# Gated linear attention feeding a two-layer feed-forward block: five hidden tiles in another form, a small copy on another engine, and a new first part of a written order

## The chip, the cores and the metric

One core of a Trainium2 chip runs the whole program. The metric is device time in microseconds (us), the median of several executions. The engines are named as in the profile: PE (TensorE, matmuls), PEld (its weight loads), DVE (VectorE), ACT (ScalarE), POOL (GpSimd), SP (SyncE, which issues nearly all transfers here).

## The reference, cut to what matters

```python
batch, n_heads, seq, head_dim = (4, 8, 768, 48)      # tokens: 3072, d_model 384, d_ff 2048
f = 1.0 / (1.0 + np.exp(-f_logit))
for t in range(S):
    state = f[:, :, t, :, None] * state + np.einsum('bhd,bhe->bhde', k[:, :, t], v[:, :, t])
    y[:, :, t] = np.einsum('bhd,bhde->bhe', q[:, :, t], state)
x = np.ascontiguousarray(attn_out.transpose(0, 2, 1, 3)).reshape(B * S, H * D)
h = x @ w_in
relu6 = np.clip(h + 3.0, 0.0, 6.0)
g = h * relu6 / 6.0
return (g @ w_out).astype(np.float32)
```

## The kernel before, in words

**Attention** is done in 24 units: a unit is 128 tokens of one batch entry, unit i belongs to token block i // 4. Each unit has a chain of small steps, named by a token `step.i`: `gate` (ACT, sigmoid), `back` (DVE, a scan that gives the product of the gates from each position to the end of the chunk), `kmul`, `rend` (DVE, the inverse of the whole chunk's product), `fwd` (DVE, a scan the other way that overwrites the first one's tile), `qmul`, then on PE `tk`, `att`, `kv`, `qs`, `av` with `ktok`, `mask`, `carry0`, `carry1`, `decay` between them, and `xh`, `xs`, `xl`, which leave the result as two float16 parts. `rend` first writes the chunk's product into the tile `ends`, clipped from below (L444, `tensor_scalar_max`), then its inverse (L445). `ends` is read later by `decay` and at the end of the program.

**Feed-forward.** The 2048 hidden values are 16 tiles of 128. A token block has 512 tokens, and one token `op.n` is tile n mod 16 of block n // 16. Float32 numbers are carried as a float16 high and low part. The first product `mm1` is 9 matmuls in float16 (three split products, three parts of the inner size). `relu` (ACT) and `g` (DVE) make the hidden value in float32, `gh` (ACT, L683) its high part, `gl` (DVE or POOL, L693) its low part, and `mm2` (L709) adds 9 float16 matmuls into three PSUM tiles `o`. In the first block, while attention still fills the machine, some tiles take another form:

- tiles 0 to 4: the 512 tokens in two halves, `mm1a` and `mm1b` (L828), `relua`/`relub`, `ga`/`gb`, and as second product `mm2a`/`mm2b` (L846), three matmuls each in float32 on the unsplit hidden value and the unsplit weights;
- tiles 5 to 7: whole tiles, with a float32 second product `mm2x` (L720), three matmuls; these need no `gh` and no `gl`;
- tiles 8 to 15 and later blocks: the split form above.

The weights are loaded by `ld` (SP) and turned into the two parts by `z`, `cy`, `high` (ACT) and `mid`, `dif`, `top`, `low` or `lowi`/`lowo` (DVE or POOL). From token block 2 on the first product is done in another way (L772, L801, L806); the change leaves it alone.

**Order.** A written list, `ORDER`, of some 1,560 tokens fixes the order on every engine and on the SP queue: each engine does its instructions in that order, and waits where an input isn't there. `ON_POOL` lists the tokens whose elementwise work goes to POOL rather than DVE. A token `warm.n` is n idle matmuls of 128 columns on PE (L1071). `outv.1` is the first token from which on the list is the same before and after, but for the inserted `ends` tokens. In the trace of before it begins at 121.18 us on DVE, and PE's next piece there, `mm1.23`, at 120.41 us.

Of the kernel before, what the change touches and what calls it, by code (L numbers as in the profile page):

```python
# [58 lines left out]
z.0 mid.0 loadq.2 gate.3 back.3 ld.1 carry0.1 warm.1 qs.1.0 dif.0 kmul.2 top.0 fwd.2 xl.0 carry1.1 loadq.3 av.1 hole.0
tk.2.4 rend.3 xh.1 xs.1 xl.1 z.1 qmul.2 warm.5 att.2.2 kmul.3 cy.1 mid.1 fwd.3 ktok.2 loadv.2 high.0 warm.4 kv.2.1  # L60
carry0.2 tk.3.4 ktok.3 mask.2 load.4 gate.4 qs.2.0 hole.1 av.2 xh.2 carry1.2 lowi.0 mm1a.0.4 relua.0 dif.1 qmul.3
top.1 high.1 ga.0 loadv.3 xs.2 att.3.2 mask.3 kv.3.1 ld.2 carry0.3 carry1.3 lowi.1 xl.2 loadq.4 warm.1 qs.3.2 av.3
xh.3 mm1a.1.4 cy.2 xs.3 xl.3 relua.1 z.2 back.4 kmul.4 rend.4 fwd.4 ga.1 decay.4 mm2a.0 qmul.4 load.5 gate.5 tk.4.1
mm2a.1 ktok.4 loadv.4 ld.3 cy.3 z.3 hole.2 mid.2 dif.2 top.2 att.4.2 kv.4.3 hole.3 mm1b.0.0 high.2 back.5 mid.3
relub.0 loadq.5 mm1b.1.1 relub.1 lowi.2 gb.0 dif.3 kmul.5 rend.5 gb.1 mm1a.2.4 mm1b.2.0 top.3 mm2b.0 mm2b.1 fwd.5
tk.5.1 relua.2 relub.2 gb.2 qmul.5 ld.4 z.4 cy.4 mid.4 mm2b.2 high.3 ktok.5 lowi.3 ga.2 mm1b.3.0 load.6 gate.6 loadq.6
dif.4 back.6 top.4 load.7 mm1a.3.4 ld.5 relub.3 mm2a.2 relua.3 ga.3 high.4 gb.3 cy.5 z.5 mask.4 mm2a.3 lowi.4 mm1a.4.1
relua.4 rend.6 ld.6 mm1b.4.4 relub.4 loadv.6 gate.7 loadq.7 mm2b.3 carry0.4 kmul.6 fwd.6 mid.5 ga.4 dif.5 z.6 qmul.6
top.5 cy.6 tk.6.1 ktok.6 mm2a.4 back.7 ld.7 decay.5 high.5 qs.4.2 decay.6 att.5.0 gb.4 av.4 kv.6.1 carry1.4 lowi.5
mm1.5.4 mask.5 mm2b.4 carry0.6 xh.4 z.7 xl.4 mid.6 dif.6 kmul.7 carry1.6 loadv.5 kv.5.3 ld.8 relu.5 g.5 mm2x.5 cy.7  # L70
top.6 high.6 cy.8 rend.7 tk.7.0 mid.7 dif.7 load.8 lowi.6 carry0.5 top.7 mm1.6.4 ktok.7 qs.5.2 fwd.7 qmul.7 high.7
loadv.7 relu.6 g.6 z.8 decay.7 att.6.0 ld.9 lowi.7 gate.8 av.5 cy.9 z.9 mask.6 mm1.7.4 relu.7 mid.8 dif.8 top.8 mid.9
carry1.5 dif.9 high.8 low.8 mm2x.6 mm1.8.0 g.7 loadq.8 ld.10 top.9 xh.5 cy.10 relu.8 high.9 back.8 rend.8 mm2x.7 ld.11
xl.5 g.8 att.7.2 z.10 cy.11 qs.6.0 kv.7.3 mid.10 load.10 loadv.8 av.6 dif.10 low.9 top.10 z.11 mid.11 gh.8 mm1.9.4
ld.12 ld.14 xh.6 xl.6 gl.8 mm2.8 dif.11 high.10 low.10 relu.9 g.9 cy.12 mm1.10.1 top.11 mask.7 kmul.8 carry0.7 gh.9
gl.9 hole.4 relu.10 high.11 mm2.9 carry1.7 g.10 low.11 z.12 mid.12 ld.13 dif.12 top.12 cy.13 gh.10 gl.10 tk.8.1 ktok.8
mm1.11.0 z.13 high.12 qs.7.2 mm2.10 av.7 loadq.9 ld.15 kv.8.3 decay.8 relu.11 mid.13 dif.13 low.12 loadv.9 mm1.12.1
g.11 gh.11 xh.7 top.13 carry0.8 high.13 xl.7 hole.7 gl.11 relu.12 z.14 z.15 low.13 fwd.8 qmul.8 mm2.11 g.12 gh.12
mm1.13.4 relu.13 g.13 cy.14 gh.13 gl.13 gl.12 mm2.12 cy.15 qs.8.2 mid.14 dif.14 att.8.0 mask.8 lowo.0 top.14 high.14
hole.6 hole.5 mm1.16.4 load.9 mid.15 mm1.17.1 relu.16 carry1.8 relu.17 dif.15 ws1.0 g.16 mm1.20.0 g.17 loadq.11 low.14  # L80
gate.10 xtop.0 gate.9 mm1.18.1 load.11 top.15 relu.18 loadq.10 back.9 high.15 gh.16 av.8 back.10 mm1.14.4 g.18 mm2.13
lowo.4 gh.17 relu.14 low.15 g.14 gh.14 mm1.15.1 mm1.19.4 lowo.6 gh.18 kmul.9 gl.18 rend.9 relu.15 g.15 lowo.3 gh.15
gl.14 gl.15 tk.9.1 lowo.5 lowo.1 mm2.14 fwd.9 mm2.15 gl.16 ktok.9 gl.17 outs.2 loadv.11 lowo.7 outv.1 outs.0 mm1.23.1
mm2.16 gate.11 lowo.2 ws2.0 relu.19 od.0 ws3.0 mm2.17 rend.10 xh.8 g.19 back.11 od.2 kmul.10 relu.20 decay.9 relu.23
kmul.11 hole.8 fwd.10 rend.11 od.1 load.13 qmul.10 xsum.0.2 g.20 g.23 mm1.21.4 relu.21 load.12 xleast.0 tk.10.3 ws4.0
qmul.9 decay.10 ktok.10 mm2.18 gh.19 g.21 mm1.25.3 gh.20 mm1.24.2 gh.21 loadv.10 gate.12 wtop.4 gl.19 relu.24 att.9.1
relu.25 kv.9.0 gl.20 fwd.11 g.25 carry0.9 loadv.12 g.24 wsh.0 load.14 qmul.11 mm1.22.4 gate.13 relu.22 back.12 gh.24
mm2.19 tk.11.3 gl.21 ws1.1 mask.9 gh.23 carry1.9 ktok.11 mm2.20 g.22 qs.9.0 att.11.3 gate.14 loadq.12 gh.25 gl.25 av.9
att.10.2 mm2.21 back.13 gh.22 xh.9 gl.23 kv.11.0 rend.12 kv.10.1 gl.22 mask.10 loadq.13 decay.11 mm1.26.4 ws2.1
mask.11 carry0.10 qs.10.3 ws3.1 carry0.11 carry1.10 kmul.12 kmul.13 fwd.12 qs.11.1 av.10 av.11 relu.26 mm2.22 ws4.1  # L90
xh.10 xh.11 decay.12 rend.13 mm1.27.3 gl.24 carry1.11 relu.27 loadq.14 decay.13 fwd.13 tk.12.2 mm1.28.1 relu.28 hole.9
ktok.12 wsl.0 ws1.2 g.27 tk.13.0 mm2.23 qmul.12 qmul.13 wsh.1 hole.10 att.13.3 ws2.2 g.26 ktok.13 g.28 xtop.1 att.12.1
t0.4 loadv.13 kv.12.2 kv.13.0 back.14 carry0.13 load.15 hole.11 load.16 xsum.1.4 carry0.12 gh.26 mm2.24 gh.27 mm2.25
t0.5 mask.13 carry1.12 t1.4 t1.5 seed.0.2 kmul.14 mm1.30.3 gh.28 t2.4 ws3.2 xleast.1 carry1.13 t2.5 th.4 ws4.2 gate.15
mask.12 gl.26 gl.27 wsl.1 th.5 ws1.3 mm2.26 tl.4 mm1.29.1 tk.14.2 relu.30 mm1.31.0 tl.5 relu.29 rend.14 g.30 p1.8.4
loadv.14 ktok.14 ws2.3 relu.31 p7.8.2 g.29 wsh.2 cs.8 ca.8.2 loadv.17 mm2.27 g.31 p6.8 gh.29 gate.16 fwd.14 qs.13.0
xtop.2 cx.8.3 qs.12.1 p2.8 wsl.2 ws3.3 ra.8 back.15 gl.28 p5.8 av.13 av.12 mm2.28 gh.31 gaw.8 loadq.15 loadq.17 gh.30
ws4.3 rend.15 load.17 ce.8 wsh.3 p4.8 qmul.14 gl.30 gl.29 xh.13 xh.12 p3.8 p8.8 rb.8 rx.8 p7.9.1 decay.14 wsl.3 mm2.29
# [1140 lines left out]
```

## Time and profile before

| | |
|---|---|
| median of 3 runs | 459.32 us (459.2 to 459.85) |
| the profiled execution's own time | 459.1 us |
| its span, first to last instruction | 457.4 us |
| outside the span | 1.7 us |
| granted TensorE clock | 1.00 of 2.4 GHz |

The profiled execution lies 0.2 us under the median. A busy PE at a granted clock of 1.00 is not yet a PE without gaps; the durations of its pieces have to be read as well.

### The profile page before, as it was taken

How to read it: one execution, taken by the hardware profiler on the slowest of the kernel's cores; microseconds unless marked ns; L12 is line 12 of the kernel's file. 1: busy time of each engine (PE TensorE's matmuls, PEld its weight loads, DVE VectorE, ACT ScalarE, POOL GpSimd, SP SyncE). 2: the span in 40 equal slices, each digit the busy share in tenths (PEclk: the TensorE clock that was granted, in tenths of full speed). 3: DMA queues.
4: the chain of work that ended last, by engine and by line, in shares of the span. 5: the costliest groups of instructions: out<-in, count | busy, mean ns of one | idle time of the engine just before them, and what ended most of it. 6: DMA issues, size and time to landing. Idle time of an engine off the chain costs nothing.

```text
span 457.4 us, 12555 instructions
## 1 busy us (share of the span) xinstructions
PE 449.4 (98%) x5445; PEld 292.8 (64%) x5449; DVE 359.3 (79%) x643; ACT 231.2 (51%) x389; POOL 19.0 (4%) x31
## 2 busy tenths in 40 slices
...
GB/s 283 223 251 385 225 189 251 203 155 16 52 125 99 158 52 59 108 3 120 89 1 85 78 142 18 21 143 2 1 10 1 5 29 2 1 115 2 1 0 73
DMA packets 25531, 43.18 MB, mean 94 GB/s; under 512 B 2560, under 2 KB 17408, under 8 KB 25472
## 3 DMA queue, kind: packets, MB, share of 16 engines
...
q14 instruction: 16, 0.13, 0.1%
...
## 4 chain that ended last, share of the span: by engine, by line
PE 94%; DVE 2%; DMA 1%; ACT 1%; issue 0%; SPq 0%; ACTq 0%
PE o L709 35%; PE pair L772 16%; PE single L772 9%; PE pair L664 7%; PE single L664 5%; PE o L846 3%; PE pair L497 3%; PE pair L587 3%; PE pair L571 3%; PE pair L537 2%; PE o L720 2%; PE pair L516 2%; PE o_half L862 1%; PE pair L862 1%; PE single L828 1%; PE pair L828 1%
## 5 line engine op out<-in xcount | busy, mean ns | idle before, releaser
L709 PE MATMUL o<-gg,weight 128*128 128x512 f16 x744 | 173.5, 379 | 0.1
L709 PEld LDWEIGHTS <-weight 128*128 128x128 f16 x744 | 71.7, 98 | 73.8
L772 PEld LDWEIGHTS <-weight 128*128 128x128 f16 x672 | 65.1, 98 | 13.3 <-issue 0.2
L772 PE MATMUL pair<-xmem,wide 128*128 128x256 f16 x384 | 51.2, 273 | 0.1
L683 ACT ACTIVATE gg<-raws 128x512 f16<-128x512 f32 x64 | 38.4, 624 | 23.9 <-DVE raws L806 8.1
L772 PE MATMUL single<-xmem,weight 128*128 128x256 f16 x384 | 49.8, 273 | 0.2 <-DVE raws L806 0.2
L801 ACT ACTIVATE raws<-pair,half 128x512 f32<-128x512 f32 x32 | 21.5, 684 | 42.7 <-PE pair L772 33.7
L772 PEld LDWEIGHTS <-wide 128*128 128x128 f16 x384 | 36.9, 98 | 8.7 <-DVE single L787 0.6
L801 ACT ACTIVATE raws<-single,half 128x512 f32<-128x512 f32 x32 | 22.0, 687 | 40.0 <-PE single L772 32.4
L664 PEld LDWEIGHTS <-weight 128*128 128x128 f16 x243 | 23.1, 98 | 26.8 <-issue 0.3
L772 PE MATMUL pair<-xmem,weight 128*128 128x256 f16 x288 | 36.5, 273 | 0.0
L806 DVE SCALAR_TENSOR_TENSOR raws<-raws,single 128x512 f32<-128x512 f32 x32 | 21.8, 682 | 18.4 <-ACT raws L801 18.4
L693 DVE TENSOR_TENSOR gg<-raws,gg 128x512 f16<-128x512 f32 x48 | 31.9, 682 | 5.0 <-ACT gg L683 5.0
L664 PE MATMUL pair<-xmem,weight 128*128 128x512 f16 x144 | 33.2, 379 | 0.0
L787 DVE TENSOR_TENSOR pair<-pair,raws 128x512 f32<-128x512 f32 x16 | 11.2, 697 | 25.5 <-PE pair L772 17.2
L806 DVE SCALAR_TENSOR_TENSOR raws<-raws,pair 128x512 f32<-128x512 f32 x32 | 21.5, 681 | 12.3 <-ACT raws L801 12.1
L448 DVE TENSOR_TENSOR_SCAN suffix<-gates,rend 112x516 f32<-112x516 f32 x24 | 29.7, 1236 | 0.1
L428 DVE TENSOR_TENSOR_SCAN suffix<-gates,unit 112x516 f32<-112x516 f32 x23 | 28.1, 1224 | 0.5 <-ACT gates L422 0.5
L664 PE MATMUL single<-xmem,weight 128*128 128x512 f16 x99 | 23.2, 380 | 0.1
L674 ACT ACTIVATE tg<-pair,half 128x512 f32<-128x512 f32 x16 | 10.9, 687 | 19.5 <-PE pair L664 16.3
L683 ACT ACTIVATE gg<-tg 128x512 f16<-128x512 f32 x24 | 14.4, 626 | 9.1 <-DVE tg L678 5.2
L504 DVE TENSOR_TENSOR a<-pair,causal 128x512 f32<-128x512 f32 x24 | 16.3, 682 | 1.2 <-PE pair L537 1.2
...
## 6 DMA issues: line engine op xcount, KB each, us to landing
...
```

The source lines that it names most:

```text
L428: nc.vector.tensor_tensor_scan(flat(sf)[:, ::-1], gt[:, 1:][:, ::-1], flat(unit)[:, ::-1], 0.0, op0=ALU.mult, op1=ALU.add,)
L448: nc.vector.tensor_tensor_scan(flat(sf), gt[:, :NP * (C + 1)], flat(rend), 0.0, op0=ALU.mult, op1=ALU.add,)
L497: nc.tensor.matmul(d["at"][HC * odd:HC * (odd + 1), e, 2 * n + c], t[rs, 1, n, c, odd], t[rs, 0, n, c, odd], start=not growing[at], stop=T ...
L504: nc.vector.tensor_tensor(d["a"].rearrange("r p e t -> r e p t"), d["at"], causal.unsqueeze(1).unsqueeze(1).broadcast_to([128, 2, NP, HC]) ...
L571: nc.tensor.matmul(d["y"][to:to + 64, odd, n, cs], before[rs, p], t[rs, 0, n, c, odd], start=alone and (odd, e) not in seen, stop=False, s ...
L664: nc.tensor.matmul(h, win[:, f, a, k * 128:(k + 1) * 128], g["xt"][:, k, :g["n"] // C, b], start=i == 0, stop=i == 3 * KT - 1,)
L683: nc.scalar.activation(d["gg"][:, 0], d["t"], AF.Copy)
L693: engine("gl", int(g["name"]) * NF + f).tensor_tensor(d["gg"][:, 1], d["t"], d["gg"][:, 0], op=ALU.subtract)
L709: nc.tensor.matmul(g["o"][m], wout[:, f, a, m * 128:(m + 1) * 128], g[f]["gg"][:, b], start=f == 0 and i == 0, stop=f == NF - 1 and i == 2 ...
L772: nc.tensor.matmul(to[:, n * 256:(n + 1) * 256], weights(q, n, a), g["wide"][:, :, block - 3, b], start=fresh and count == 1, stop=count = ...
L801: nc.scalar.activation(to, src, AF.Relu, bias=half, scale=RISE)
L806: nc.vector.scalar_tensor_tensor(to, to, TOP, src, op0=ALU.min, op1=ALU.mult)
```

## The change

Tiles 3 to 7 of the first block take the split form (`mm1`, `relu`, `g`, `gh`, `gl`, `mm2`) in place of the halves (3 and 4) or the float32 second product (5 to 7). The copy of the chunk's product into `ends` goes to ACT as a step of its own, without the clip; DVE's inverse reads the scan's result directly. The list before `outv.1` is another one; `ON_POOL` has 5 tokens in place of 15. Lines from 445 on move by 2 to 4.

```diff
 ON_POOL = """
-kmul.1 decay.4 kmul.6 lowi.5 kmul.7 decay.7 lowi.7 kmul.8 gl.9 decay.8 gl.11 qmul.8 gl.12 lowo.0 low.14
+lowi.2 gl.3 lowo.5 qmul.6 low.9
 """.split()
 ORDER = """
...
+mm1.6.4 ktok.7 qs.5.2 fwd.7 qmul.7 high.7
...
+        def close():
+            nc.scalar.activation(ends[:, i], sf[:, :, 0], AF.Copy)
+
         def turn():
-            nc.vector.tensor_scalar_max(ends[:, i], sf[:, :, 0], END_LIMIT)
-            nc.vector.reciprocal(rend[:, :, 0], ends[:, i])
+            nc.vector.reciprocal(rend[:, :, 0], sf[:, :, 0])
...
-            "kmul": kmul, "rend": turn, "fwd": forward,
+            "kmul": kmul, "ends": close, "rend": turn, "fwd": forward,
```

On PE, at the second product of tile 5 (`tg_5` is its float32 hidden value, `gg_5` its two float16 parts, `o` the three output tiles, `wide` the unsplit and `weight` the split weights), before:

```order
L537 MATMUL pair_71<-v_912,ktok_714 48x48
L720 MATMUL o_0_572<-tg_5_931,wide 128x512
L720 MATMUL o_1_573<-tg_5_931,wide 128x512
L720 MATMUL o_2_574<-tg_5_931,wide 128x512
L516 MATMUL pair_70<-ident,qkf_792 128x112 x4
```

and now the first six of eighteen rows, three rounds of them in all:

```order
L713 LDWEIGHTS weight
L713 MATMUL o_0_622<-gg_5_924,weight 128x512
L713 LDWEIGHTS weight
L713 MATMUL o_1_623<-gg_5_924,weight 128x512
L713 LDWEIGHTS weight
L713 MATMUL o_2_624<-gg_5_924,weight 128x512
```

Three float32 matmuls have become nine float16 ones, which also wait for `gg`.

On DVE, the rows up to the second `ga` (the 37th to 48th row of its program in both), that is the end of the start-up (L428 is `back`, L448 `fwd`, L841 `ga`, L301, L308 and L312 `mid`, `dif`, `top` of a weight tile, L441 `kmul`, L504 `mask`, L320 a low part), before:

```order
L308 TENSOR_TENSOR top_377<-top_377,raws 128x768
L454 TENSOR_TENSOR qkf_325<-qkf_325,suffix_77 112x512
L312 SCALAR_TENSOR_TENSOR wide<-top_377,wide 128x2x384
L841 SCALAR_TENSOR_TENSOR th_0_461<-th_0_461,single 128x256
L504 TENSOR_TENSOR a_488<-pair_71,causal 128x2x4x64
L320 TENSOR_TENSOR weight<-wide,weight 128x384
L428 SCALAR_TENSOR_TENSOR suffix_79<-gates_78,unit 112x516
L441 TENSOR_TENSOR qkf_519<-qkf_519,suffix_79 112x512
L444 TENSOR_SCALAR ends<-suffix_79 112x4
L445 RECIPROCAL rend<-ends 112x4
L448 SCALAR_TENSOR_TENSOR suffix_79<-gates_78,rend 112x516
L841 SCALAR_TENSOR_TENSOR th_1_562<-th_1_562,single 128x256
```

and now (line numbers 2 to 4 higher):

```order
L310 TENSOR_TENSOR top_408<-top_408,raws 128x768
L443 TENSOR_TENSOR qkf_373<-qkf_373,suffix_79 112x512
L314 SCALAR_TENSOR_TENSOR wide<-top_408,wide 128x2x384
L449 RECIPROCAL rend<-suffix_79 112x4
L303 TENSOR_SCALAR raws<-top_542 128x768
L452 SCALAR_TENSOR_TENSOR suffix_79<-gates_78,rend 112x516
L310 TENSOR_TENSOR top_542<-top_542,raws 128x768
L322 TENSOR_TENSOR weight<-wide,weight 128x384
L314 SCALAR_TENSOR_TENSOR wide<-top_542,wide 128x2x384
L845 SCALAR_TENSOR_TENSOR th_0_589<-th_0_589,pair_70 128x256
L458 TENSOR_TENSOR qkf_373<-qkf_373,suffix_79 112x512
L845 SCALAR_TENSOR_TENSOR th_1_616<-th_1_616,pair_70 128x256
```

The steps of a third weight tile (`top_542`) and the `qmul` of unit 4 have come ahead of the second `ga`, and the first `ga`, which was the fourth of these rows, is now the tenth.

On ACT, the start of its program after the first two sigmoids, before:

```order
L422 ACTIVATE gates_78<-gates_78 112x4x128
L523 ACTIVATE ktok_156<-pair_71 128x448
L550 ACTIVATE middle_102<-pair_70 112x2x2x48
L422 ACTIVATE gates_80<-gates_80 112x4x128
L608 ACTIVATE xmem<-pair_71 112x4x128
L523 ACTIVATE ktok_243<-single 128x448
```

and now:

```order
L446 ACTIVATE ends<-suffix_77 112x4
L424 ACTIVATE gates_78<-gates_78 112x4x128
L527 ACTIVATE ktok_162<-single 128x448
L446 ACTIVATE ends<-suffix_79 112x4
L424 ACTIVATE gates_80<-gates_80 112x4x128
L424 ACTIVATE gates_76<-gates_76 112x4x128
L554 ACTIVATE middle_102<-pair_71 112x2x2x48
```

The copies (L446) stand between the sigmoids, and the sigmoid of the fourth unit (the second `gates_76`) has moved ahead of the first `carry0` (`middle_102`).

## Rows read from the trace of the kernel before

**Rows 1.** Page, part 1: engine, busy us (share of the span), instructions.

```profile
PE 449.4 (98%) x5445; PEld 292.8 (64%) x5449; DVE 359.3 (79%) x643; ACT 231.2 (51%) x389; POOL 19.0 (4%) x31
```

**Rows 2.** Windows: length, busy (instructions) of PE, PEld, DVE, ACT, POOL, clock, DMA.

```profile
3.50:31.30 27.80, 25.09 (x581) 16.94 (x580) 25.56 (x42) 16.37 (x32) 2.05 (x3) 1.00 0.80 296
31.30:121.20 89.90, 89.90 (x1034) 54.36 (x1033) 81.95 (x142) 61.73 (x95) 14.41 (x14) 1.00 0.50 182
121.20:250.00 128.80, 128.64 (x1812) 81.40 (x1812) 118.45 (x213) 64.49 (x112) 0.00 (x0) 1.00 0.27 84
```

**Rows 3.** Chain that ended last, 30 to 82 us: start, us, what.

```profile
32.95 1.48 PE o L846 x6
...
35.06 0.44 PE pair L537 x26
...
37.57 0.98 PE single L828 x9
...
39.53 2.59 PE o L846 x12
...
67.98 2.58 PE o L720 x6
70.55 1.94 PE pair L664 x9
...
79.10 1.94 PE o L709 x9
```

**Rows 4.** Lines by form, DVE, 31.3 to 121.2 us: count, busy us, mean ns, idle before.

```profile
L312 DVE SCALAR_TENSOR_TENSOR wide<-top,wide 128x768 int16<-128x768 int16 x14 | 14.3, 1024 | 0.1
L308 DVE TENSOR_TENSOR top<-top,raws 128x768 int16<-128x768 int16 x14 | 7.8, 555 | 0.3
...
L320 DVE TENSOR_TENSOR weight<-wide,weight 128x384 f16<-128x384 f32 x10 | 5.4, 553 | 0.2 <-ACT weight L317 0.2
L693 DVE TENSOR_TENSOR gg<-tg,gg 128x512 f16<-128x512 f32 x8 | 5.3, 683 | 0.8 <-ACT gg L683 0.7
L301 DVE TENSOR_SCALAR raws<-top 128x768 int16<-128x768 int16 x14 | 4.9, 350 | 0.1
L678 DVE SCALAR_TENSOR_TENSOR tg<-tg,single 128x512 f32<-128x512 f32 x7 | 4.8, 685 | 3.4 <-ACT tg L674 3.4
...
L841 DVE SCALAR_TENSOR_TENSOR th<-th,single 128x256 f32<-128x256 f32 x4 | 1.6, 410 | 0.3 <-ACT th L837 0.3
L441 DVE TENSOR_TENSOR qkf<-qkf,suffix 112x512 f32<-112x512 f32 x2 | 1.4, 684 | 0.0
...
L444 DVE TENSOR_SCALAR ends<-suffix 112x4 f32<-112x4 f32 x5 | 0.8, 162 | 0.0
L457 DVE TENSOR_TENSOR decayed<-state,ends 112x192 f32<-112x192 f32 x2 | 0.7, 350 | 0.0
```

**Rows 5.** Timeline of DVE, 112 to 123 us: start, us, what.

```profile
116.24 1.29 DVE L693 TENSOR_TENSOR gg<-tg,gg 128x512 f16<-128x512 f32 x2
```

**Rows 6.** Timeline of all engines, 0 to 36 us.

```profile
2.98 0.20 ACT L253 ACTIVATE table<-half 128x1 f32<-128x1 f32 x1 [0.89 <-POOL half L251]
...
8.05 1.23 DVE L428 TENSOR_TENSOR_SCAN suffix<-gates,unit 112x516 f32<-112x516 f32 x1 [0.51 <-ACT gates L422]
...
9.50 1.42 POOL L441 TENSOR_TENSOR qkf<-qkf,suffix 112x512 f32<-112x512 f32 x1 [5.76 <-DMA qkf<-qk]
...
9.79 1.16 DVE L444 TENSOR_SCALAR ends<-suffix 112x4 f32<-112x4 f32 x1
...
27.24 0.42 DVE L841 SCALAR_TENSOR_TENSOR th<-th,single 128x256 f32<-128x256 f32 x1 [0.97 <-ACT th L837]
```

**Rows 7.** Waits of DVE, 31.3 to 121.2 us: waited for, us in total, times, longest.

```profile
DVE tg L678 <- ACT tg L674: 4.5, 6, 2.4
```

**Rows 8.** Timeline of PE, 118 to 124 us.

```profile
120.41 2.11 PE L664 MATMUL pair<-xmem,weight 128*128 128x512 f16 x9
```

More of the change, by code (lines that the diff above doesn't have):

```diff
@@ L59 @@
[L59 to L98, printed above, removed]
@@ new lines @@
+top.2 ga.0 loadq.6 gate.5 qmul.4 warm.1 relua.1 ga.1 cy.3 z.3 mm2a.0 back.5 decay.4 mid.3 cy.4 mm2a.1 gate.6 carry0.4
+z.4 dif.3 carry1.4 mm1b.0.0 top.3 carry1.3 ends.5 back.6 high.3 lowi.3 mid.4 mm1b.1.1 ld.5 att.4.2 relub.0 gb.0 load.7
+dif.4 mm1.3.4 ends.6 high.2 ld.6 kmul.5 relub.1 mask.4 lowi.2 relu.3 gb.1 mm2b.0 loadv.5 rend.5 mm1a.2.0 top.4 fwd.5
+z.5 cy.5 high.4 mid.5 mm1b.2.2 qmul.5 lowi.4 ld.7 tk.5.3 mm1.4.1 g.3 lowo.3 relua.2 dif.5 relub.2 mm2b.1 gate.7
+loadq.7 gh.3 relu.4 ld.8 cy.6 gb.2 ga.2 mm2b.2 g.4 loadv.6 top.5 z.6 ktok.5 mid.6 qs.4.0 gl.3 kmul.6 high.5 dif.6 gh.4
@@ new lines @@
+decay.5 top.6 back.7 att.5.3 lowi.5 cy.7 ld.9 high.6 kv.5.1 av.4 z.7 carry0.5 mask.5 tk.6.4 cy.8 mm2a.2 mm2.3 lowo.6
+mid.7 mm1.5.2 kmul.7 z.8 dif.7 lowo.5 lowo.4 lowi.6 mid.8 top.7 ktok.6 relu.5 high.7 mm1.6.3 g.5 gh.5 gl.4 lowi.7
+mm2.4 rend.6 cy.9 loadv.8 z.9 carry1.5 gl.5 dif.8 relu.6 decay.6 loadq.8 top.8 fwd.6 tk.7.2 mid.9 ld.10 xh.4 mm1.7.4
+ktok.7 relu.7 g.6 high.8 z.10 gh.6 qmul.6 loadv.7 g.7 dif.9 low.8 mm2.5 gl.6 cy.10 rend.7 ends.7 top.9 high.9 fwd.7
+qs.5.1 att.6.3 kv.6.2 carry0.6 mask.6 ld.11 av.5 ld.12 carry1.6 low.9 xl.4 load.9 mm1.8.4 mid.10 cy.11 loadq.9 xh.5
```

130 lines of the change are left out of this document (81 added, 49 removed).

## The prediction

> **What bounds the kernel now.** I read the page's busy times first: PE is busy 98% of the span, DVE 79% [rows 1]. A mean over the span hides the stages, so next the windows [rows 2]. From 31.3 to 121.2 us, the stretch in which the new list takes effect after the start-up, PE is busy 89.90 of 89.90 us: there is no gap in it to win, only work to take out. DVE, second, is busy 81.95 us of it, so it has 7.95 us to spare. Behind 121.2 us PE is again full (128.64 of 128.80) and DVE at 118.45. Before 31.3 us things are different: PE works 25.09 of 27.80 us, part of it idle matmuls, and DVE 25.56; there the chain of the first attention units sets the pace, and DVE is its busiest engine. The chain that ended last [rows 3] runs from 31 us on through one matmul group after another. So the reader should look for three things: how much PE work goes, what the start-up gives, and whether DVE, which takes over work, can follow.
>
> **PE work that goes.** A float32 second product takes 2.58 us whole and 2.59 us in two halves; the split one takes 1.94 us [rows 3]. The two half-size first products take 0.98 us each, the whole one 1.94: no difference. Three tiles give 3 x 0.64 us and two give 2 x 0.65 us: **3.2 us** less on PE, which has nothing to hide it under in this stretch. The rows are of the same shapes, so I give this term no range.
>
> **The start-up.** Its end is the second `ga` on DVE, which frees PE's second `mm2a` (at 32.95 us, [rows 3]). Pieces on DVE that follow each other overlap a little: two low parts of 0.683 us take 1.29 us together [rows 4, 5], so each further one costs its mean less 0.08 us. Ahead of that `ga` there come in, by [rows 4]: `kmul.1` from POOL 0.60, `mid` 0.27, `dif` 0.47, `top` 0.94 of the third weight tile, and `qmul.4`, of the shape of `kmul`, 0.60: 2.9 us. Out go five `ends` pieces, four of 0.16 us and one that took 1.16 us: 1.8 us. Two waits also end: 0.51 us of the second unit's scan, since `qmul.0` now stands ahead of it, and 0.97 us of the first `ga`, which now comes six pieces later [rows 6]. Net the second `ga` comes 2.9 - 1.8 - 1.5 = -0.4 us, so 0.4 us earlier. PE has by then also done `kv.4` (0.44 us, [rows 3]), which stood behind it. I take **0.8 us**. Lower bound -0.7: both waits come back elsewhere. On the SP queue, one v load of 128 x 400 floats has moved ahead of the second unit's q and k; at 296 GB/s [rows 2] it delays them by 0.7 us, from the 9.50 us at which POOL got them [rows 6] to 10.2 us. DVE comes to `kmul.1` at about 10 us by the sum of the pieces before it, so this costs at most some 0.3 us, inside the bound. The later loads move to earlier places among pieces that wait for them less than in the list of before; I cost them at nothing, under the cover of DVE's own queue.
>
> PE alone would thus come to `mm1.23` at 120.41 [rows 8] - 3.2 - 0.8 = 116.4 us: a limit of 4.0 us.
>
> **What DVE takes on.** Up to `outv.1` it does 7 more `gl` (five tiles more, two fewer on POOL: 15 for 8) at 0.60 us, 4 more `kmul` at 0.60, 3 more `decay` at 0.27, one more `lowi` at 0.47; four half-size `ga`/`gb` of 0.33 become two whole `g` of 0.60 (-0.1); ten `ends` go, nine at 0.16 and one at 1.16 us (-2.6) [rows 4, 6]. That is 4.2 + 2.4 + 0.8 + 0.5 - 0.1 - 2.6 = **+5.2 us**. From 3.5 to 121.2 us DVE was busy 25.56 + 81.95 = 107.5 of 117.7 us and idle 10.2 us. To arrive 4.0 us earlier it must do 112.7 us of work in 113.7 us: 1.0 us of idle time is left. The start-up keeps some 0.75 us (2.24 less the 1.5 above), so 0.25 us remains for a stretch that had 7.95.
>
> That price is between two ends. If DVE never waits longer than that, the gain is 4.0 us. If it waits there as long as before, and PE waits for every bit, the gain is 4.0 - 7.7 = -3.7 us. The largest part of those waits, 4.5 us in six pieces, is DVE at `g` waiting for ACT's `relu` of a matmul group just done [rows 7]: the wait of an engine that is ahead of PE. With 98% of its time full DVE is mostly behind, and such waits shrink. So I take the value near the first end: 1.7 us of idle time, which costs **1.5 us**.
>
> **What is cheap.** The copy into `ends` has no row on ACT. The nearest are ACT's 128 x 1 piece at 0.20 us [rows 6] and DVE's 112 x 192 `decay` at 0.35 us [rows 4]; I take 0.2, it is that small. Ten copies and five `gh` (no longer than `gl`, 0.68 us) are 5.4 to 7 us more on an ACT that idles 28 of 89.9 us [rows 2]. The cover is this idle time; if it were gone, each copy would delay the `relu` or sigmoid behind it by 0.2 us. The Trainium skill speaks against this part: in "ScalarE: Activation LUTs", "Rules for kernel authors", it gives relu, max, min, add and mul to VectorE and budgets about 0.3 us for every activation. By that an estimate for 24 copies is 7.2 us, by the row 4.8 us, and either fits in ACT's idle time.
>
> The `ends` piece of 1.16 us began while POOL's `kmul.1` ran, and ended with it, at 10.95 and 10.92 us [rows 6]; the same piece alone takes 0.16. I count this 1.0 us as gone, since that POOL piece is. If it were chance, and came back on another piece, the sum would be 1.0 us worse. By the Trainium skill ("SBUF — State Buffer", "Who interferes with whom") it isn't chance: VectorE and GpSimd share a port pair, and the second to come is blocked until the first has finished; the trace agrees at this place.
>
> Behind `outv.1` PE's work is the same and full, DVE loses fourteen `ends` (2.2 us) and has 10.35 us to spare up to 250 us [rows 2], in which it can work off a lag. I take nothing there, bounds -0.4 and +0.4 us.
>
> **Sum.** 3.2 + 0.8 - 1.5 = 2.5 us off the profiled execution's 459.1 us: 456.6. The median of before lies 0.2 us higher, so for a median I say **456.8 us**.
>
> **Rivals.**
> - *DVE eats the gain.* At about 4.2 us of idle time on DVE between 31 and 117 us, half of what was there, nothing is left: 459.3. For it: work and time on PE and DVE now match to 1 us. Against: the waits seen are those of an engine ahead.
> - *DVE becomes the bound and the kernel is slower.* DVE is in order; each time it comes to `g` before ACT's `relu` is there, everything behind it, now also `gl`, `kmul` and `decay`, is late, and with them the low parts that the last third of each `mm1` and `mm2` reads. It decides from 4.2 us up; with the whole 7.95 us it gives 459.3 + 3.7 = 463.0. POOL, which took some of this load, is used for 5 pieces instead of 15.
> - *The scan waits for the copy.* `fwd` overwrites the tile that ACT's copy reads, so it must wait for ACT's queue up to the copy; behind `fwd` DVE's whole queue stands. If each of ten early copies sat behind one piece of 0.7 us, DVE would lose 7 us, near the rival before: some 461 to 462. Against: in the list other DVE pieces (`kmul`, `qmul`, `mid`) stand between `rend` and `fwd` in nearly every unit, and ACT is the less busy engine.
> - *No waits at all*: 455.3.
>
> **How the numbers follow.** I give the forecast (a gain of 1 to 3.9 us: 455.4 to 458.3) 0.65, the eaten gain 0.18, DVE as the bound 0.10, the scan behind the copy 0.04, no waits 0.03. The range 455.0 to 460.2 leaves out the two slower cases' far ends and little else, under 2 in 10; the forecast's own is 455.4 to 458.3. A difference of 0.2%, 0.9 us, is about the least that this measurement can tell. Faster than that: the forecast and no waits, 0.68. Within: 0.18. Slower: 0.14.
>
> **What would show it.** Right: tiles 3 to 7 with nine matmuls of 1.94 us in all, no float32 group after tile 2; PE at `mm1.23` between 116.5 and 119 us and full from 32 us on but for 1 to 2 us; DVE over 97% busy in that stretch, with `g` waiting for ACT under 2.5 us; the second `mm2a` before 32.95 us; from `outv.1` to the end the same 336.2 us within 0.5. Wrong: idle time on PE between 32 and 117 us of over 3 us released by DVE's low parts, `kmul` or `qmul`; `fwd` waiting for ACT; a start-up whose second `mm2a` comes after 33.5 us; a granted clock under 1.00 anywhere.

## The result

The changed kernel is 0.8% slower: 462.88 us (461.56 to 463.0, 4 runs) against 459.26 us (4 runs), a ratio of 1.0077 with a 95% interval of 1.0065 to 1.0090. The forecast was 456.8 us, faster. The profiled execution took 461.56 us with a span of 459.8; before it was 459.1 and 457.4. So the trace shows 2.4 us of the loss; the other three runs took some 1.3 us more, at mean clocks of 0.991 to 0.995 (0.994 in the trace), which the clock alone does not explain.

The busy times and windows of the changed kernel, with the columns of [rows 1, 2]:

```profile
PE 448.8 (98%) x5450; PEld 290.8 (63%) x5450; DVE 360.4 (78%) x632; ACT 234.9 (51%) x416; POOL 9.6 (2%) x21
```

```profile
3.50:31.30 27.80, 24.16 (x577) 17.92 (x576) 23.38 (x37) 16.27 (x35) 0.24 (x1) 0.94 0.79 285
15.00:20.00 5.00, 3.69 (x62) 3.01 (x66) 3.78 (x7) 2.90 (x7) 0.00 (x0) 0.77 1.03 407
20.00:25.00 5.00, 4.57 (x137) 3.60 (x132) 4.09 (x6) 3.02 (x7) 0.00 (x0) 0.89 0.41 160
31.30:121.20 89.90, 87.60 (x1029) 50.33 (x1028) 86.27 (x148) 63.51 (x103) 6.87 (x5) 1.00 0.54 186
121.20:250.00 128.80, 128.80 (x1814) 81.34 (x1812) 115.92 (x201) 64.72 (x120) 0.00 (x0) 1.00 0.26 81
```

Against [rows 2], DVE has lost 2.2 us of work in the start-up (23.38 for 25.56), PE now idles 2.3 us between 31.3 and 121.2 us, and the granted clock is at 0.77 and 0.89 of 2.4 GHz between 15 and 25 us, where it was 1.00. Page and windows tell where to look; the timelines tell why. PE (the first three lines are of the kernel before, for the end of its start-up; the others are of the changed kernel):

```profile
32.87 1.56 PE L846 MATMUL o<-th,wide 128*128 128x256 f32 x6
34.36 0.69 PE L497 MATMUL pair<-qkf 48*64 48x64 f32 x32
34.88 0.62 PE L537 MATMUL pair<-v,ktok 64*64 64x48 f32 x32
```

```profile
15.68 0.34 PE L575 MATMUL pair<-qkf,middle 48*64 48x64 f32 x6
17.18 0.44 PE L575 MATMUL pair<-qkf,middle 48*64 48x64 f32 x10 [1.16 <-issue]
...
19.02 1.13 PE L501 MATMUL pair<-qkf 48*64 48x64 f32 x32
19.92 1.40 PE L541 MATMUL pair<-v,ktok 64*64 64x48 f32 x48
...
23.09 0.33 PE L591 MATMUL pair<-a,v 64*48 64x64 f32 x7 [0.43 <-issue]
...
35.05 2.86 PE L850 MATMUL o<-th,wide 128*128 128x256 f32 x12
37.74 2.13 PE L832 MATMUL pair<-xmem,weight 128*128 128x256 f16 x18
...
90.24 4.04 PE L668 MATMUL pair<-xmem,weight 128*128 128x512 f16 x18 [1.98 <-DMA xmem<-xmem]
...
122.79 2.11 PE L668 MATMUL pair<-xmem,weight 128*128 128x512 f16 x9
```

In the middle of one `qs`, PE stands for 1.16 us for nothing that the profile shows ("issue"). From 17.71 to 21.12 us the granted clock is then at half, 1.2 GHz: the 32 matmuls of `att` take 1.13 us, where they take 0.69 at the full clock. DVE (the first line, its second `ga`, is of the kernel before; the others are of the changed kernel):

```profile
32.42 0.39 DVE L841 SCALAR_TENSOR_TENSOR th<-th,single 128x256 f32<-128x256 f32 x1
```

```profile
6.30 0.69 DVE L443 TENSOR_TENSOR qkf<-qkf,suffix 112x512 f32<-112x512 f32 x1 [1.21 <-DMA qkf<-qk]
...
20.29 0.69 DVE L508 TENSOR_TENSOR a<-pair,causal 128x512 f32<-128x512 f32 x1 [1.47 <-PE pair L501]
...
25.71 0.69 DVE L508 TENSOR_TENSOR a<-pair,causal 128x512 f32<-128x512 f32 x1 [1.34 <-PE pair L501]
...
35.19 0.41 DVE L845 SCALAR_TENSOR_TENSOR th<-th,pair 128x256 f32<-128x256 f32 x1
```

Two masks wait 2.8 us for PE, and the first `kmul` waits 1.21 us for its keys (0.29 before). The second `ga` comes at 35.19 us; before it came at 32.42, and the forecast, 0.4 us earlier, had it at 32.0. From there the chain that ended last, in order of time, no longer runs through PE as in [rows 3]:

```profile
42.42 0.60 DVE a L508
43.51 0.76 issue
44.27 1.21 DVE suffix L452
...
59.31 0.94 DVE wide L314
60.25 0.56 DVE tg L682
60.81 0.60 DVE gg L697
...
84.38 0.84 DVE weight L322
85.22 0.61 DVE xmem L626
85.85 0.56 SPq L633
86.46 3.64 DMA xmem<-xmem
90.24 4.04 PE pair L668 x18
```

But for some 4 us on ACT from 73 us on, it goes nearly piece by piece through DVE up to `xl.7` (L626), from there through the transfer `hole.7`, which moves the odd heads of unit 7 to their place, and ends in PE's wait of 1.98 us at 90.24, the first tile of token block 1. From `outv.1` on everything lies 2.4 us later than before, to the end.

The account, by starts on PE. After its second `mm2a` PE went on at 34.36 us before and at 37.74 now; it has then also done `kv.4`, which took 0.55 us behind that place (from 34.88 to the next piece at 35.43), so the start-up is 2.8 us longer. From there to `mm1.23` it took 86.05 us before ([rows 8] less 34.36) and 85.05 now; less the 0.55 us and the two waits now there (1.98 and 0.16 us), the work itself is 2.6 us shorter. 2.8 + 2.1 - 2.6 = +2.3 us, of 2.4.

### The profile page after: what moved, and what is told of

Read it like the earlier page. It is cut to its first block, busy times and chain, and to the rows that moved or that the text cites. A ratio compares the mean times of both kernels' runs of the same rounds, so it can differ in the third digit from the quotient of the medians.

```text
span 459.8 us, 12561 instructions
## 1 busy us (share of the span) xinstructions
PE 448.8 (98%) x5450; PEld 290.8 (63%) x5450; DVE 360.4 (78%) x632; ACT 234.9 (51%) x416; POOL 9.6 (2%) x21
## 4 chain that ended last, share of the span: by engine, by line
PE 82%; DVE 11%; issue 2%; DMA 2%; ACT 1%; SPq 0%; DVEq 0%; ACTq 0%
PE o L713 34%; PE pair L776 16%; PE single L776 9%; PE pair L668 6%; PE pair L501 2%; PE pair L591 2%; PE pair L575 2%; PE pair L541 2%; PE single L668 2%; DVE weight L322 1%; DVE wide L314 1%; PE pair L520 1%; DVE suffix L430 1%; PE pair L866 1%; PE o_half L866 1%
## 5 line engine op out<-in xcount | busy, mean ns | idle before, releaser
L713 PE MATMUL o<-gg,weight 128*128 128x512 f16 x789 | 184.0, 379 | 0.0
L713 PEld LDWEIGHTS <-weight 128*128 128x128 f16 x789 | 76.1, 98 | 78.7
L776 PEld LDWEIGHTS <-weight 128*128 128x128 f16 x672 | 65.1, 98 | 13.3 <-issue 0.2
L687 ACT ACTIVATE gg<-raws 128x512 f16<-128x512 f32 x64 | 38.4, 624 | 23.8 <-DVE raws L810 8.1
L668 PE MATMUL pair<-xmem,weight 128*128 128x512 f16 x189 | 43.6, 379 | 2.0 <-DMA xmem<-xmem 2.0
L668 PEld LDWEIGHTS <-weight 128*128 128x128 f16 x261 | 24.6, 98 | 31.0 <-issue 2.8
L678 ACT ACTIVATE tg<-pair,half 128x512 f32<-128x512 f32 x21 | 14.3, 685 | 26.6 <-PE pair L668 23.3
L687 ACT ACTIVATE gg<-tg 128x512 f16<-128x512 f32 x29 | 17.4, 624 | 6.3 <-PE o L713 5.7
L697 DVE TENSOR_TENSOR gg<-tg,gg 128x512 f16<-128x512 f32 x28 | 18.6, 681 | 0.0
```

What stands on the lines that cost most here:

```text
L668: nc.tensor.matmul(h, win[:, f, a, k * 128:(k + 1) * 128], g["xt"][:, k, :g["n"] // C, b], start=i == 0, stop=i == 3 * KT - 1,)
L678: nc.scalar.activation(d["t"], d["h"], AF.Relu, bias=half, scale=RISE)
L687: nc.scalar.activation(d["gg"][:, 0], d["t"], AF.Copy)
L697: engine("gl", int(g["name"]) * NF + f).tensor_tensor(d["gg"][:, 1], d["t"], d["gg"][:, 0], op=ALU.subtract)
L713: nc.tensor.matmul(g["o"][m], wout[:, f, a, m * 128:(m + 1) * 128], g[f]["gg"][:, b], start=f == 0 and i == 0, stop=f == NF - 1 and i == 2 ...
L776: nc.tensor.matmul(to[:, n * 256:(n + 1) * 256], weights(q, n, a), g["wide"][:, :, block - 3, b], start=fresh and count == 1, stop=count = ...
```

## The experiments

Each kernel was run beside the kernel before, whose median was 458.85 to 459.16 us. Order edits are shown by the tokens concerned; `...` stands for tokens left as they are.

**Is it the new start? Graft the old one.** The tokens up to `mm2a.1` are put in the order of the kernel before, with their warm units and loads, `kmul.1` and `decay.4` on POOL. (In e1 unit 3's second carry reads its PSUM bank after it was used again, so that one attention state differs; the work is the same.) e5 puts this carry back in its old place, moves one backward scan with its copy ahead, and leaves `decay.4` on DVE (the tokens of the scan and the copy):

```diff
-av.3 xh.3 mm1a.1.4 cy.2 xs.3 xl.3 relua.1 z.2 back.4 kmul.4 ends.4 rend.4 fwd.4 ga.1 decay.4 mm2a.0
+av.3 xh.3 back.4 ends.4 mm1a.1.4 cy.2 xs.3 xl.3 relua.1 z.2 kmul.4 rend.4 fwd.4 ga.1 decay.4 mm2a.0
```

> The changed kernel, with the steps up to the second mm2a of the first pass in the order of before (its warm tokens, its loads, kmul.1 and decay.4 on GpSimd again); the rest of the list is the new one. Theory (most of the loss is the new start-up: the first mm2a comes at 35.05 us for 31.27, less 0.4 us for kv.4 done ahead, 3.4 us in all): 459.5 us, TensorE's granted clock 1.00, the 2.0 us wait for the hole transfer near 88 us still there. Rival (VectorE's added work is the bound, and the start-up's loss would only be made up for by it): 462 to 463, with VectorE's queue late behind 40 us.

> The changed kernel with the old start up to the second mm2a, as in e1_old_start, but with the copy of chunk 4's end put right behind its backward scan (there it stood behind three other ScalarE pieces, and the forward scan waited 2.42 us for it) and the second carry of unit 3 in its old place. If the new start loses the 3.35 us, this gives 459.5 to 460.3, with the first mm2a near 31.5 and no halved clock in the first 35 us. If the rest of the new order needs the new start (its buffers and queues), the time stays at 462 or more although mm2a comes early. e1 changed two things at once, so it did not tell these apart.

Measured: e1 464.58 us (ratio 1.0121, 1.0104 to 1.0137), e5 467.37 (1.0168, 1.0128 to 1.0208). Both are slower than the changed kernel. In e1 the forward scan waits for the copy on ACT, the third rival of the prediction, which the new order avoids:

```profile
33.87 1.23 DVE L451 TENSOR_TENSOR_SCAN suffix<-gates,rend 112x516 f32<-112x516 f32 x1 [2.42 <-ACT ends L445]
```

In e5 the first whole tile's `mm1` waits instead, by the list of PE's waits (us in total, times, longest):

```profile
PE single L667 <- ACT weight L318: 4.3, 1, 4.3
```

Two orders sewn together give a new queue on ACT and DVE at the seam, so these runs do not tell what the new start costs, although in both the first `mm2a` comes at 31.8 us, near the 31.5 that was forecast for e5. The same two with the earlier `xl.7` of e2 (below) took 466.49 and 467.39 us (e3 and e6); 457 to 457.5 and 457.3 to 458.5 had been forecast, for two losses that add.

**The transfer.**

```diff
-xh.7 top.12 low.11 high.12 mm1.11.0 hole.6 xl.7 relu.9 low.12 g.9 cy.13 z.14 g.10 back.9 hole.7
+xh.7 xl.7 hole.7 top.12 low.11 high.12 mm1.11.0 hole.6 relu.9 low.12 g.9 cy.13 z.14 g.10 back.9
```

> The changed kernel with xl.7 and hole.7 moved right behind xh.7, nothing else. Theory (the 2.0 us in which TensorE waits for the hole transfer of unit 7 is a term of its own): 460.9 us, and no wait of TensorE for a transfer near 88 us. Rival (VectorE is the bound there; the wait hides another for its low parts): 462.5 or more, with TensorE waiting for gl or low in the same place.

Measured: 461.73 us (1.0053, 1.0031 to 1.0075). DVE, in order, stands 1.54 us at the early `xl.7` for ACT, and PE's wait has another name at the same place:

```profile
89.69 6.65 PE L668 MATMUL pair<-xmem,weight 128*128 128x512 f16 x30 [1.80 <-DVE weight L322]
```

So the edit trades the wait for one of nearly the same length that it makes itself; what the transfer's wait alone costs is not shown. (The profiled run is the slowest of e2's five, 463.54 us, with half the clock from 23.8 to 30.7 us; three runs at 0.999 or more took 460.8 us on average, but the changed kernel has no such run to set beside them.) How long PE waits here differs from trace to trace: the four last issues on SP take the same 3.5 us, but from the first of them to PE's start it was 6.74 us in the changed kernel, 5.75 in e14, 5.00 in e4 and 4.99 in e16 (below), with a wait of 1.98, 1.01, 0.24 and 0.24 us.

**The clock.** e4 adds two warm units to the changed kernel. e13 takes all but the first two warm tokens out of the kernel before (three of the eight places are shown):

```diff
-qmul.0 tk.0.4 gate.1 ... carry1.1 av.0 rend.2
+qmul.0 tk.0.4 warm.4 gate.1 ... carry1.1 av.0 warm.2 rend.2
```

```diff
-qmul.0 warm.1 att.0.0 ... gate.2 warm.1 av.0 ... qmul.1 warm.3 att.1.0
+qmul.0 att.0.0 ... gate.2 av.0 ... qmul.1 att.1.0
```

> The changed kernel with a warm.4 behind tk.0 and a warm.2 behind av.0, in places where TensorE idles 1.4 and 0.5 us; nothing else. Theory (the 3.4 us at half clock from 17.7 us on are a part of the start-up's loss, some 1.2 us of longer matmuls, which work in those gaps prevents): clock 1.00 throughout and 461.3 to 461.8 us. Rival (the start-up is set by VectorE's and the transfers' chain, or the extra warm work lies on the path itself): same time, 462.5 to 463.5, whatever the clock.

> The kernel before without its warm units from the third on (11 of its 31 matmuls without a result; the order of all else unchanged), so that TensorE has gaps in the start and no other change. This prices the clock alone: if gaps in the start make the clock fall as in the changed kernel, the clock is 0.990 to 0.996 and the time 460.5 to 463, with the first mm2a late by half the stretch at the half clock; if the clock holds without them, 458.5 to 459.3, and the fall in the changed kernel has another cause than TensorE's gaps.

Measured: e4 461.82 us (1.0072, 1.0049 to 1.0094); the clock of its profiled run is 1.000, but in its other runs 0.993 to 0.996, and PE's stop is longer than in the changed kernel:

```profile
22.93 0.42 PE L591 MATMUL pair<-a,v 64*48 64x64 f32 x11 [2.53 <-issue]
```

So the two warm units change nothing that the ratio can tell, and the run that held the clock stopped for 2.53 us all the same.

e13 462.20 us (1.0074, 1.0046 to 1.0102), at clocks of 0.978 to 0.989 in all runs. Its windows, where all but the gaps is the kernel before:

```profile
15.00:20.00 5.00, 2.98 (x81) 1.93 (x72) 4.93 (x10) 2.65 (x7) 0.00 (x0) 0.87 0.23 87
20.00:25.00 5.00, 3.87 (x96) 3.31 (x100) 4.58 (x10) 3.51 (x7) 0.00 (x0) 0.50 0.83 261
25.00:31.30 6.30, 5.66 (x155) 4.32 (x147) 3.30 (x6) 3.67 (x9) 0.00 (x0) 0.69 0.84 320
```

PE is busy 2.98 of 5 us, and the clock is at half from 18.70 to 28.94 us, all of the second window. One of the gaps is a stop of 0.87 us, up to 16.16, that the kernel before does not have ("issue"). So gaps in the start bring the clock down, and gaps, stop and half clock together cost 3.0 us; the runs do not part them. Over the runs of several kernels, by their mean clock:

| kernel | clock 0.998 or more | below |
|---|---|---|
| before, beside e12 | 14 runs, 458.47 to 459.73 us | 3 runs (0.996), 460.39, 460.93, 461.86 |
| changed | none | 4 runs, mean 462.6 |
| e12 | 3 runs, mean 459.8 | 9 runs, mean 462.5 |
| e14 | 4 runs, mean 459.9 | 6 runs, mean 461.7 |
| e16 | 9 runs, mean 459.2 | 2 runs, mean 461.4, and one of 467.67 |
| e17 | 9 runs, mean 459.0 | 3 runs, mean 462.2 |

In each kernel that has both, a fallen clock goes with 1.8 to 3.2 us more. No trace shows what else differs in those runs.

**The stops, and the loads.** e7 gives the kernel before five of the early loads of the changed one, and nothing else:

```diff
-loadq.3 hole.0 loadv.2 load.4 hole.1 loadv.3 ld.2 loadq.4
+loadq.3 loadv.2 load.4 ld.2 loadq.4 loadv.3 hole.0 hole.1
```

> The kernel before with one thing of the new start alone: five loads (values 2 and 3, gates 4, weights 2, queries and keys 4) are issued ahead of the first head transfer, as the changed kernel does. Theory: while all 16 DMA engines are busy TensorE's instructions come late. Then between 15 and 22 us waits of TensorE for nothing shown (issue) of 1 to 2.5 us each appear in an order of work that had none, the first mm2a slips from 31.1 to about 32 to 33 us, and the time is 460 to 462. Rival: TensorE's stops come from the many small matmuls and warm units of the new start; then the early loads change nothing (458.5 to 459.3).

Measured: 458.73 us (1.0000, 0.9984 to 1.0016): nothing, though the DMA engines are now full from 15 to 20 us (1.03 in the last column but one; the first line is of the kernel before, the second of e7):

```profile
15.00:20.00 5.00, 4.76 (x108) 3.11 (x107) 4.93 (x9) 3.10 (x8) 0.00 (x0) 1.00 0.26 98
15.00:20.00 5.00, 4.61 (x108) 3.18 (x108) 4.97 (x10) 2.82 (x7) 0.00 (x0) 1.00 1.03 415
```

Full DMA engines alone do not stop PE. Then loads of the changed kernel were moved, its order otherwise kept (tokens of SP's queue alone; e10 is e9 with `xl.7` on DVE ahead of `low.11`, one piece earlier, and `hole.7` behind `hole.6`; e15 is e14 with the warm units of e4, e16 is e15 with its own loads):

```diff
 changed: loadv.1 load.2 loadq.1 loadv.3 load.3 loadq.2 loadq.3 ld.0 loadv.2 load.4 ld.1 ld.2 loadq.4 hole.0 loadv.4 load.5
+e9:      loadv.1 load.2 loadq.1 load.3 loadq.2 loadq.3 ld.0 loadv.2 load.4 ld.1 loadv.3 hole.0 loadq.4 ld.2 loadv.4 load.5
+e12:     load.2 loadq.1 loadv.1 ld.0 load.3 loadq.2 loadq.3 ld.1 loadv.2 load.4 load.5 loadv.3 loadq.4 ld.2 hole.0 loadv.4
+e14:     load.2 loadq.1 loadv.1 ld.0 load.3 loadq.2 loadq.3 ld.1 loadv.2 load.4 load.5 loadv.3 loadq.4 hole.0 ld.2 loadv.4
+e16:     load.2 loadq.1 loadv.1 ld.0 load.3 loadq.2 loadq.3 loadv.2 ld.1 load.4 load.5 loadv.3 ld.2 hole.0 loadq.4 loadv.4
```

> The changed kernel with three loads of the start later and nothing else moved: values 3 behind weights 1, and queries and keys 4 and weights 2 behind the first head transfer. Theory: in the new start TensorE reaches its row 357 (about 20.0 us) before the instructions for it have come, since their transfer starts at 20.3 to 20.7 us there, behind full DMA engines, against 17.5 in the kernel before and 19.3 in e7_before_early_loads, whose TensorE gets to that row after 22 us. Neither the loads alone (e7) nor the order alone does it. Then the wait for nothing shown of 0.4 to 2.5 us at 20 to 23 us goes, the clock is not halved, VectorE's masks no longer wait 2.8 us for TensorE, and the second mm2a comes at 32.5 to 33.5 in place of 36.4: 459.8 to 460.8. Rivals: weights 2 or keys 4 now come late themselves and take the place of the stop (462.5 and more); or the stops belong to the order of the matmuls (clock 0.99 again, 462.5 to 463).

> e9_late_loads with the low part of unit 7 on VectorE one piece earlier (ahead of a weight's low half of 0.95 us, not at once behind the high part as in e2_hole_early, where VectorE stood 1.54 us for ScalarE) and its transfer right behind. The first tile of block 1 waits 1.98 us for that transfer: 0.3 to 0.95 us under e9 if the transfer starts as much sooner, the same as e9 if the two issues of the transfer ahead of it on SyncE's queue set its start.

> The changed kernel with its start's loads in an order near the old one's, paced: values 1 behind keys 1, weights 1 ahead of values 2, and values 3, keys 4 and weights 2 behind gates 5, whose own wait for chunk 2's forward scan (17.4 us) holds them back. In e9_late_loads the engines were still at 0.79 from 15 to 20 us, TensorE's instructions for row 357 began to come at 19.6 us and TensorE stood 1.7 us, then ran 5 us at the half clock; and weights 2, issued at 25 us, came late in e10. Theory: what sets the stop is the load on the DMA engines between 15 and 20 us. With the engines free at 17 us the transfer starts at 17.5 to 18.5 us, the stop is under 0.5 us, the clock stays at 0.998 or more, and the time is 457.5 to 460. Rival: the new order has TensorE at row 357 too soon whatever the loads do, or the late keys and weights cost as much: a stop of 1 us and more or other waits, the clock at 0.993 to 0.996 and 462 to 465.

> e12_loads_paced with weights 2 (768 KB) behind the first head transfer. In e12 the stop at row 357 had gone (0.28 us at row 228 only), but the loads let go at 17.4 us kept the engines at 0.92 from 20 to 25 us, and TensorE stood 2.4 us one block of instructions later, at row 486, whose transfer began at 25.1 us. Theory: with only 0.7 MB let go at 17.4 us both stops stay under 0.6 us, the clock is at 0.998 or more in most runs, and the median is 458.7 to 460 (the two runs of e12 at a clock of 1.000 took 458.99 and 459.20). Rival: weights 2 then come late for ScalarE, as in e10 (TensorE 2.1 us at 27 us), the clock falls behind that wait, and the median is 461 to 464.

> e14_weights_last with the two extra warm units of e4_more_warm (six matmuls without a result, 0.7 us behind the first product of attention and two more behind the first transposes). If the fall of the clock is the larger part of the loss, the same median as e14 or 0.5 to 1 us less, with fewer runs under 0.998; if the warm units only lengthen TensorE's row, 0.3 to 0.7 us more than e14.

> e15_weights_last_warm with weights 2 ahead of the first head transfer and keys 4 (512 KB, needed on VectorE only at 27 to 29 us) behind it in their place, and values 2 ahead of weights 1. In e14 and e15 no stop for instructions was left, but TensorE waited 1.4 to 1.5 us at 29 us behind ScalarE, which waited for weights 2, and 0.6 to 0.7 us for values 2; the first mm2a came at 34.7 to 35.5 us. Theory: without these two waits it comes at 32.5 to 33.3 us, which is the start of the forecast, and the runs with a clock of 0.998 or more take 457.0 to 458.5, the median 457.5 to 459.5. Rival: 0.97 MB let go at 17.4 us delays the instructions for row 486 again as in e12 (a stop of 1 us or more at 25 us, clock 0.993 to 0.996), or keys 4 come late: 460 to 463.

Measured, medians: e9 464.11 us (1.0079 to 1.0145), e10 463.89 (1.0073 to 1.0139), e12 461.90 (1.0026 to 1.0078), e14 460.91 (1.0026 to 1.0059), e15 460.45 (1.0025 to 1.0063), e16 459.83 (1.0014, 0.9998 to 1.0030). e9 and e10 missed their forecasts, and e10's earlier `xl.7` gained nothing over e9. Where PE stops in them is seen in a queue of the trace that moves nothing but instructions, in 43 transfers of 16 KB. That they are PE's is inferred: PE has some 10,960 rows in the trace, 255 for each transfer, and its stops always fall behind the same rows, 228, 357 and 486 of its weight loads and semaphore instructions, counted from the start of the program; these lie 129 apart, with 127 matmuls between:

```text
kernel    transfer starts   PE at the row   goes on   start to go
changed   14.77  (row 228)      15.74        17.18        2.41
changed   20.73  (row 357)      22.39        23.09        2.36
e2        20.25  (row 357)      20.38        22.70        2.45
e4        20.35  (row 357)      20.13        22.93        2.58
e9        19.55  (row 357)      19.97        21.91        2.36
e12       25.14  (row 486)      24.90        27.59        2.45
e16       23.44  (row 486)      24.74        25.79        2.35
before    17.46  (row 357)      23.09        no stop
e7        19.32  (row 357)      22.40        no stop
e12       17.69  (row 357)      21.00        no stop
e14       17.32  (row 357)      20.55        no stop
```

In all 18 stops of this kind in the first 36 us, in twelve kernels, PE goes on 2.2 to 2.6 us after that transfer starts, and where it gets to the row later than that it does not stop. Two things make a stop: the new order brings PE to row 357 some 2 to 3 us sooner than the old one did (in the changed kernel itself the half clock took that back), and full DMA engines delay the transfer's start, from 17.3 to 18.3 us to 19.3 to 20.7. e7 has only the second, e14 only the first. e12 shows both sides in one kernel: row 357 is free, but the loads let go at 17.4 us fill the engines at 0.92 between 20 and 25 us, and the next stop is there (the share alone does not tell it: at 0.89 in e17 that transfer started at 22.90 us, without a stop):

```profile
27.59 0.62 PE L541 MATMUL pair<-v,ktok 64*48 64x48 f32 x14 [2.44 <-issue]
```

e14 has no stop, but pays, as its rival said, with weights that come late to ACT (L612 waits in ACT's queue behind them):

```profile
28.97 0.43 PE L616 MATMUL pair<-xmem,less 112*112 112x256 f16 x2 [1.42 <-ACT xmem L612]
```

The stops alone do not order the times either: e10's is 0.83 us, but PE then waits 2.1 us for late weights. e16 is left with stops of 0.16 and 0.79 us; its first `mm2a` comes at 33.92 us (its forecast was 32.5 to 33.3), its second `ga` at 34.05. By its ratio it lies 0.6 us over the kernel before (-0.1 to 1.4): loads and two warm units, with the order of all work kept, take back 2.9 of the 3.5 us by which the changed kernel's ratio lies over it. It is no faster than the kernel before. (e15 against e14: with the warm units 7 of 12 runs held the clock, without 4 of 10.)

**The parts by themselves.** e8 is the kernel before with tiles 5 to 7 alone in the split form; e11 the kernel before with the copy of the ends on ACT, right behind each backward scan:

```diff
-relu.5 g.5 mm2x.5 cy.7 top.6 high.6 cy.8 ... top.7 mm1.6.4
+relu.5 g.5 gh.5 cy.7 top.6 high.6 lowo.5 gl.5 cy.8 ... top.7 mm2.5 mm1.6.4
```

```diff
-load.1 fwd.0 gate.1 back.1 warm.16
+load.1 fwd.0 gate.1 back.1 ends.1 warm.16
```

> The kernel before with tiles 5 to 7 alone as whole split products (nine fp16 matmuls in place of three fp32), nothing else moved but the low halves that they need. By the term of the prediction TensorE has 3 times 0.64 = 1.9 us less to do, at six more pieces on VectorE (some 3.6 us) in a stretch where VectorE is idle 2 us of 30: 457 to 458.5 if the copies hide, 459 to 460 if VectorE takes it back.

> The kernel before in its own order with the change's other part alone: the copy of a chunk's ends goes from VectorE to ScalarE, right behind the chunk's backward scan. The term of the prediction is nought (0.2 us for a copy on either engine): 458.7 to 459.4. If ScalarE then stands for the scan with other work behind it, or the forward scan waits for ScalarE as in e1_old_start (2.42 us), 460 to 463.

Measured: e8 464.37 us (1.0124, 1.0107 to 1.0141), e11 464.97 (1.0141, 1.0121 to 1.0161). e8's clock is 1.00 in the trace, and PE waits between 60 and 90 us for what the split needs of ACT and DVE:

```profile
PE pair L664 <- ACT weight L317: 2.8, 1, 2.8
PE single L664 <- DVE tg L678: 1.9, 1, 1.9
PE pair L497 <- DVE xmem L622: 1.6, 1, 1.6
```

In e11 one forward scan waits 2.4 us for ACT. `tg` waits 4.7 us in six pieces, but that is no loss of e11: it was 4.5 us in six before [rows 7]. All five of its runs have a fallen clock (0.989 to 0.996), so its price holds some of that too. Neither part is nearly free in an order that was not made for it. This does not price them in the new order; it shows that the order has to pay for both.

**Is it DVE then?** e16 with four pieces on POOL:

```diff
-lowi.2 gl.3 lowo.5 qmul.6 low.9
+lowi.2 gl.3 lowo.5 qmul.6 low.9 kmul.6 lowi.5 kmul.7 decay.7
```

> e16_keys_last with four pieces of VectorE (kmul 6 and 7, decay 7 and a half low part of weights 5) on GpSimd, as in the kernel before; the order is the same. In e16 and the changed kernel the chain runs piece by piece through VectorE from about 49 to 85 us (in the kernel before through TensorE), and VectorE is busy 57.6 of 58.7 us there. Theory: with the start mended VectorE is the bound in that stretch, and takes back the 2.9 us that TensorE was relieved of. The four pieces are 0.60 + 0.60 + 0.27 + 0.47 = 1.9 us of its queue, so with a held clock 457.3 to 458.5, a median of 457.5 to 459. Rival: what GpSimd does comes later than VectorE needs it (1.2 us a piece for 0.6), or the bound is still the start: 459.5 to 461.

Measured: 459.52 us (1.0018, 0.9997 to 1.0040), with a held clock 459.0 on average (e16: 459.2), where 457.3 to 458.5 was forecast. No gain to speak of. `xl.7` comes at 84.35 us in place of 84.94, 0.6 us sooner for 1.9 us of relief, and as much sooner the second `ga` came in this trace already (33.48 for 34.05). The chain now runs through PE from 72.5 to 83.7 us before it comes to `xl.7` and the transfer. So the theory that DVE's queue alone is the bound there is not confirmed.

## Why the prediction was wrong, by its own steps

- **PE work that goes, -3.2 us:** right. Tiles 3 to 7 run as nine matmuls of 1.94 us and no float32 group stands after tile 2. By starts, behind the second `mm2a`, 13.2 us of float32 second products gave way to 10.1 us of float16 ones: 3.1 us. Small pieces took back some 0.5, so that the stretch is 2.6 us shorter without its waits.
- **The start-up, -0.8 us:** this step failed. It came out at +2.8. The sum went over DVE's pieces alone, with PE on time and the later loads "at nothing, under the cover of DVE's own queue". The pieces were near what was counted, and the two waits of 0.51 and 0.97 us did end; but new ones came. PE was not on time: 1.16 and 0.43 us of stops, 3.4 us at half clock, hence 2.8 us of masks waiting; and the first keys came 0.9 us later. 35.19 less these is 31.5 us, and in e4, e9, e12 and e14 to e17 the second `ga` less the waits that DVE has beyond the 0.29 us of before lies at 31.4 to 31.8 us too, with 1.8 to 5.6 us of such waits. So the sum of the pieces holds, 0.2 to 0.6 us under the forecast's 32.0, and what failed is that the new start was taken to be free of waits. How much of the late first keys belongs to the new order is open: their transfer is issued at 1.73 us in every trace, and they land between 5.7 and 6.7 us where the start is the new one, between 5.5 and 6.4 where it is the old one. The loads, which I looked at for the data they bring, also did harm by what they delay: PE's instructions. "A granted clock under 1.00 anywhere" was named as a sign, but no rival had a price for it.
- **What DVE takes on, cost 1.5 us:** right in kind, near in size. PE waits 2.1 us between 32 and 91 us, at the end of a chain through DVE. I had put its sign at `g` waiting for ACT under 2.5 us (it was 3.2; [rows 7] had 4.5) and at DVE busy for over 97% (96%); the cost showed as a late `xl.7` and its transfer, which had no term. How much of it is DVE's is open: in e16 `xl.7` comes only 0.2 us sooner, and PE waits 0.24 us there.
- **The cheap part, 0 us:** held in the new order (a copy takes 0.19 to 0.25 us on ACT, no scan waited for it), and not in two others (2.4 us each in e1 and e11). The rival was right about the mechanism.
- **Behind `outv.1`, 0 us:** right; the lag stays at 2.4 us.

The rival "DVE eats the gain", 459.3 us, has the number that e16 and e17 come to when the clock holds, 459.2 and 459.0, but that is not its mechanism: their start-up is still late. Two times of PE account for the traces of the new order: where PE goes on behind its second `mm2a`, and what it waits from there to 126 us. The span less both is 419.9 to 420.2 us in all ten kernels that have that order from the start on, and 422.5 in the kernel before, if its `kv.4` (0.55 us) is counted to the start-up:

```text
kernel    PE goes on   over before   later waits   span
before       34.91         -            0.0        457.4
changed      37.74        2.8           2.1        459.8
e12          39.96        5.1           0.9        461.0
e14          38.17        3.3           1.2        459.2
e16          37.56        2.7           0.4        457.8
e17          36.74        1.8           2.0        458.7
```

So the saved work, 2.3 to 2.6 us, is there in all ten, and the start-up is never where the forecast had it. It is late even in e17, which has no stop and held its clock: there DVE waits 2.1 us for keys in two places, and PE 0.53 us for the transfer of odd heads that the first `mm1b` needs. In e16 that wait is

```profile
37.56 2.13 PE L832 MATMUL pair<-xmem,weight 128*128 128x256 f16 x18 [0.78 <-DMA xmem<-xmem]
```

That the order of the loads (with two warm units) decides over most of the 3.5 us is shown by e16. That they are the stops and the half clock of the start is not: the traces of e16 and of the changed kernel lie 1.9 us apart, and of that the start-up is 0.2 us and the wait for `hole.7` 1.7. What stops and half clock do is shown inside the start (the masks' 2.8 us) and, in the old order, by e13. Open stay the 1.3 us by which three runs of the changed kernel were slower than its trace, and why the wait at `hole.7` differs so between traces: from `xl.7` to PE's start it is 5.1 us in the changed kernel, 4.8 in e17, 4.1 in e14 and 3.4 in e16.
